# First V of the first batch in two groups of loads, and three zero blocks less ahead of the first scores

## The chip, the cores and the metric

The kernel runs on one NeuronCore of one Trainium2 chip. Its engines work side by side and meet through semaphores: TensorE (PE, with its weight loads listed as PEld) multiplies matrices, VectorE (DVE), ScalarE (ACT) and GpSimd (POOL) work on vectors, SyncE (SP) issues stores. Loads and stores are carried by 16 DMA engines; in this kernel POOL issues all loads and SP all stores. The metric is the time of one execution in microseconds (us) on the device, taken as the median of several runs.

## The reference

Two steps follow each other. Attention over 8 batches, 12 heads, 448 tokens and 64 numbers a head, and then a feed-forward layer over the 3584 tokens with 768 numbers each:

```
scores = scale * q @ k.T                  # per batch and head, scale = 1/sqrt(64)
attn   = softmax(scores)
x      = (attn @ v)  as [3584, 768]       # heads side by side
h      = x @ w_in                         # w_in 768 x 2048
g      = h * (1 / (1 + exp(-h)))
out    = g @ w_out                        # w_out 2048 x 768
```

The inputs and the output are 32-bit floats in memory. The loads turn the inputs into 16-bit floats on their way, the products take those and add up in 32 bits. Sizes of loads are given as they are written, in 16 bits.

## The kernel before

**Tiling.** A unit is one batch and one group of four heads (`HG = 4`, three groups a batch, `NG = 3`). For a unit the kernel loads K, Q and V, turns K and Q with VectorE's 32 x 32 transposes (lines 407, 412, 424), multiplies them to scores in 32-row strips of TensorE (`scores`, line 460), takes the exponential on ScalarE (`expo`, lines 505 and 516), and multiplies the exponentials with V and with ones (`attend_alone`, line 568, for the first units, line 582 later). VectorE turns and inverts the sums (lines 640, 648, 655) and scales the product into `xT` (lines 674 and 685), which is the left side of the feed-forward layer (`h<-xT,w_in_t`, line 697).

**Scores.** The scores of batch 0 come in bursts; each burst fills two score tiles of PSUM, and ScalarE takes one exponential for each. There are three such tiles at this stage, so a burst waits for the exponential that frees its tile.

**V.** All V of a batch lies in one tile `V` of 128 partitions by 12 heads by 4 chunks by 64. One load brings one quarter of the partitions, 32, for some heads, with 4 or 3 tokens in each partition, which is 64 or 48 KB for four heads (`load_v`, lines 351 to 366). `plan_v` queues four such loads, x = 0 to 3; for batch 0 they take all 12 heads at once (192 and 144 KB), for later batches one group of four heads. `lift_v` (lines 369 to 376) moves one chunk of the second group between partitions on VectorE, and clears what it came from; it needs the first two quarters of V.

**The order of the work.** A planner writes all instructions in a fixed order ahead of time. The class `Order` keeps a clock and an estimate for every engine, and emits an operation when its estimate says that it can start. `od.load` puts a load in POOL's list with its rows and bytes; when the planner reaches it, it calls the emit function that was given with it. Loads go out in the order in which they were planned (lines 1216 to 1243): K of unit 0, its Q in two halves, K and Q of unit 1, K of unit 2, then V of batch 0, Q of unit 2, K and Q of batch 1's first unit, six pieces of `w_in`, and so on. The planner holds at most eight loads in flight (`LOADS = 8`, line 23), and so does the program: a load waits on POOL for the landing of the load eight before it, because they share a semaphore.

**Zero blocks.** Where TensorE would wait at the start, the planner puts products of zeros (`run_zeros`, line 2329), which write to a spare bank and are read by nobody. The first group has `FIRST` blocks of 128 columns, four to a product; later groups are as long as the wait that the planner expects:

```
each = mm(128) if od.now > COLD else 0.107
n = max(1, int((wait - 0.06) / each), int(wait / each + 0.9) * (od.now < COLD))
wide = 4
if warm.pop("first", None):
    n, wide = FIRST, 4
```

Of the kernel before, what the change touches and what calls it, by code (L numbers as in the profile page):

```python
# [214 lines left out]
def kernel(  # L215
# [11 lines left out]
    B, NH, S, D = q.shape  # L227
# [3 lines left out]
    NG = NH // HG  # L231
# [15 lines left out]
    EAGER = 1  # L247
    HALVES = 0
    NEAR, LATE = 0.15, -0.3
    COLD, FIRST, QUIET = 8.5, 47, 0.16  # L250
    SHY = 0.5
    AWAIT = 1.0
    FAR = (NT * B // 4 - 1,)
# [86 lines left out]
    def form(b, hg):  # L340
        return "low" if b == 0 else ("low", "high")[(NG * b + hg) % 2]
# [9 lines left out]
    def load_v(b, hg0, hg1, x):  # L351
        if b not in VT:
            VT[b] = sb.tile([128, NH, NCH, D], FP16, name=f"V_{b}", tag="V", bufs=2)
        hs = slice(HG * hg0, HG * hg1)
        kind = form(b, hg0)
        if x == 0 and b > 0 and NG * b + hg0 < ALONE:
            lo = 64 if kind == "low" else 0
            nc.gpsimd.memset(VT[b][lo : lo + 64, hs, place(b, hg0, NCH - 1), :], 0.0)
        first, count = X_TOK[kind][x]
        at = int(kind == "high" and count < NCH)  # L360
        nc.gpsimd.dma_start(  # L361
            out=VT[b][32 * x : 32 * (x + 1), hs, at : at + count, :],
            in_=v[b, hs].rearrange("h (i g) d -> i h g d", g=TPP)[
                :, :, first : first + count, :
            ],
        )
# [88 lines left out]
    def place(b, hg, c):  # L455
        return (c + 1) % NCH if form(b, hg) == "high" else c
# [714 lines left out]
    od = Order(SHY)  # L1171
# [10 lines left out]
    def plan_q(n):  # L1182
# [7 lines left out]
            for g0, g1 in (PIECES if n == 0 else ((0, TPP),))  # L1190
        ]

    def plan_v(b, hg0, hg1):
        made = []
        for x in range(4):
            ring = v_ring if (x == 0 and hg0 == 0) else None
            heads, toks = HG * (hg1 - hg0), X_TOK[form(b, hg0)][x][1]
            made.append(
                od.load(32 * heads, 2 * D * toks, lambda x=x: load_v(b, hg0, hg1, x), ring)
            )  # L1200
        for hg in range(hg0, hg1):
            ld_v[(b, hg)] = made
# [16 lines left out]
    plan_q(1)  # L1219
    plan_k(0, 2)  # L1220
    plan_v(0, 0, NG)
    plan_q(2)
    plan_k(1, 0)
# [7 lines left out]
    plan_q(5)  # L1231
    plan_w_out(0, 4)
    plan_v(1, 0, 1)
    plan_w_out(4, 8)
    plan_w_out(8, 12)
    plan_v(1, 1, 2)
    plan_w_out(12, 16)
    plan_v(1, 2, 3)
    for n in range(NB0 + NG, NU):
        b, hg = units[n][:2]  # L1240
# [1186 lines left out]
```

## Time and profile before

| what | us |
|---|---|
| median of 3 runs | 377.55 (377.43 to 378.58) |
| profiled execution | 377.82 |
| its span | 376.0 |
| PE busy | 370.4 |
| DVE busy | 292.4 |
| ACT busy | 255.6 |
| POOL busy | 85.0 |

The span is the time from the first to the last instruction of the profiled execution; the execution's own time has some 1.8 us more around it. A line of the timeline or of the chain begins with the start and the duration in us, then the engine, the line of the kernel, the operation, what it writes and reads, and how often it was done in one stretch; the square bracket tells how long the engine sat idle before it, and what ended that. A row of a group has the busy time, the mean duration in ns, and the idle time before. `rk` and `room` are raw K, `rq` is raw and turned Q, `KT` is turned K, `s` the scores, `E` and `T` the exponentials, `a` the product with V or with ones, `z` the bank of the zero blocks and whatever takes it over, `rdn` the sums. A load has landed when all its 16 engines have reported; "to landing" counts from its issue on POOL.

### The profile page before, as it was taken

What the parts mean: (1) busy time and instruction counts of PE and PEld (TensorE: products, weight loads), DVE (VectorE), ACT (ScalarE), POOL (GpSimd) and SP (SyncE); (2) the same over time, 40 slices, a digit from 0 to 9 for tenths busy, and PEclk for the clock granted to TensorE, in tenths of its full rate; (3) what the DMA queues carried; (4) which work ended last, traced back from release to release, by engine and by line L of the source; (5) the groups of instructions that cost most, each with busy time, mean ns of one, the idle gap of its engine ahead of it and who ended that gap; (6) DMA issues with size and microseconds to landing.
All of it is one profiled execution on the core that took longest, in us unless ns stands there. A gap on an engine that the chain in (4) does not pass through costs nothing.

```text
span 376.0 us, 10031 instructions
## 1 busy us (share of the span) xinstructions
PE 370.4 (98%) x4052; PEld 189.3 (50%) x4052; DVE 292.4 (78%) x613; ACT 255.6 (68%) x402; POOL 85.0 (23%) x155
## 2 busy tenths in 40 slices
PE   8999999999999999999999999999999999999996
PEld 3365445444444444444444444545556765556774
DVE  3667958999995969995969998899579744648883
ACT  4988873887878788777878777658872238883121
POOL 7552437424016326006423200000000000000000
PEclk9999999999999999999999999999999999999999
DMA  7999999919049948147964421210001241000144
GB/s 112 198 208 210 206 204 183 199 18 135 14 99 137 171 51 120 30 94 106 171 97 57 60 53 45 53 34 0 0 3 46 63 107 39 0 3 26 50 115 150
DMA packets 35967, 34.49 MB, mean 92 GB/s; under 512 B 11856, under 2 KB 35152, under 8 KB 35920
## 3 DMA queue, kind: packets, MB, share of 16 engines
q0 software_dynamic: 25312, 22.82, 41.1%
q1 hardware_dynamic: 10064, 10.40, 10.2%
q8 instruction: 32, 0.52, 0.6%
q10 hardware_dynamic: 544, 0.62, 0.5%
q14 instruction: 15, 0.12, 0.1%
HBM read 45.61 MB, written 11.01 MB: 151 GB/s over the span
## 4 chain that ended last, share of the span: by engine, by line
PE 97%; DMA 1%; issue 0%; POOL 0%; DVE 0%; POOLq 0%
PE p L697 28%; PE h L697 21%; PE f L697 16%; PE s L460 12%; PE a L582 8%; PE o L697 3%; PE a L568 2%; PE n_Q L697 2%; PE a L615 2%; PE n_P L697 2%; DMA rq<-in_q_dram 1%; PE z L2329 1%; PE z L697 0%; PE z L568 0%; DVE ost L1033 0%
## 5 line engine op out<-in xcount | busy, mean ns | idle before, releaser
L516 ACT ACTIVATE E<-s 128x896 f16<-128x896 f32 x164 | 142.0, 919 | 24.8 <-PE s L460 24.7
L697 PE MATMUL h<-xT,w_in_t 128*32 128x448 f16 (+2 forms) x762 | 83.5, 348 | 0.0
L697 PEld LDWEIGHTS <-w_in_t 128*128 128x128 f16 (+1 forms) x909 | 54.6, 97 | 50.0 <-issue 8.1
L361 POOL DMA_DIRECT2D V<-in_v_dram x88 | 48.5, 565 | 49.7 <-PE a L582 29.2
L697 PEld LDWEIGHTS <-G 128*128 128x128 f16 (+1 forms) x652 | 40.1, 97 | 26.0 <-issue 5.0
L729 ACT ACTIVATE th<-h 128x448 f16<-128x448 f32 x67 | 36.6, 546 | 24.3 <-PE h L697 20.7
L697 PE MATMUL p<-w_out_t,G 128*128 128x384 f16 (+1 forms) x294 | 46.7, 327 | 0.0
L460 PE MATMUL s<-rq,KT 32*128 32x448 f16 (+3 forms) x728 | 44.9, 347 | 0.5 <-DVE rq L424 0.5
L697 PEld LDWEIGHTS <-S 128*128 128x128 f16 (+1 forms) x329 | 29.9, 98 | 21.3 <-issue 3.4
L773 DVE SCALAR_TENSOR_TENSOR G<-th,h 128x448 f16<-128x448 f16 (+1 forms) x64 | 35.7, 573 | 4.7 <-ACT th L729 4.3
L697 PE MATMUL p<-D,S 128*128 128x384 f16 (+1 forms) x217 | 39.3, 327 | 0.0
L1027 ACT COPY ost<-p 128x384 f32<-128x384 f32 x36 | 17.3, 480 | 26.8 <-PE p L697 24.2
L582 PE MATMUL a<-E,V 128*32 128x448 f16 (+1 forms) x640 | 32.7, 356 | 0.0
L685 DVE SCALAR_TENSOR_TENSOR xT<-a,rdn 128x448 f16<-128x448 f32 x46 | 26.9, 618 | 3.4 <-PE a L582 2.2
L338 POOL DMA_DIRECT2D rq<-in_q_dram x25 | 13.9, 558 | 67.0 <-PE s L460 58.2
L460 PEld LDWEIGHTS <-KT 32*128 32x128 f16 (+1 forms) x824 | 12.4, 96 | 31.0 <-issue 29.2
L529 DVE TENSOR_TENSOR T<-T,E 128x1792 f16<-128x1792 f16 x21 | 22.8, 1086 | 4.8 <-ACT E L516 4.8
L529 DVE TENSOR_TENSOR T<-E,E 128x1792 f16<-128x1792 f16 x21 | 22.7, 1082 | 4.1 <-ACT E L516 4.0
L901 DVE TENSOR_TENSOR p<-f,p 128x448 f32<-128x448 f32 x15 | 9.3, 623 | 20.3 <-PE f L697 13.9
L1049 DVE TENSOR_TENSOR ost<-p,ost 128x384 f32<-128x384 f32 x28 | 15.4, 552 | 12.2 <-ACT ost L1027 7.7
L697 PE MATMUL f<-sx,tw 128*128 128x448 f16 x102 | 23.7, 353 | 0.0
L582 PEld LDWEIGHTS <-V 128*32 128x32 f16 (+1 forms) x640 | 13.5, 95 | 18.0 <-issue 10.1
(140 smaller groups left out, 483.9 us busy)
## 6 DMA issues: line engine op xcount, KB each, us to landing
out_dram<-ost SPq DMA_DIRECT2D x146, 48.0 KB, 2.2
rk<-in_k_dram POOLq DMA_DIRECT2D x23, 224.0 KB, 5.3
rq<-in_q_dram POOLq DMA_DIRECT2D x23, 224.0 KB, 5.9
w_out_t<-in_moe_w_out_dram POOLq DMA_DIRECT2D x4, 768.0 KB, 12.6
V<-in_v_dram POOLq DMA_DIRECT2D x42, 64.0 KB, 4.4
out_dram<-wide SPq DMA_DIRECT2D x48, 48.0 KB, 1.6
V<-in_v_dram POOLq DMA_DIRECT2D x42, 48.0 KB, 4.6
w_in_t<-in_moe_w_in_dram POOLq DMA_DIRECT2D x6, 256.0 KB, 9.2
```

Source lines behind the costliest of these rows:

```text
L338: nc.gpsimd.dma_start(out=rawq[n][:, cols], in_=group_of(q, b, hg)[:, cols])
L361: nc.gpsimd.dma_start(out=VT[b][32 * x : 32 * (x + 1), hs, at : at + count, :], in_=v[b, hs].rearrange("h (i g) d -> i h g d", g=TPP)[:, : ...
L460: nc.tensor.matmul(out=pS[p0 : p0 + 32 * (x1 - x0), h % 2, at : at + q1 - q0], lhsT=KT[(b, hg)][32 * h : 32 * (h + 1), key_rows(b, hg, c, ...
L516: nc.scalar.activation(out=E[(n, w)][:, 2 * y : 2 * y + 2, :], in_=pS_t[(n, w, y)][:, :, 0:S], func=AF.Exp, scale=attn_scale,)
L529: nc.vector.tensor_tensor(out=T[n], in0=T[n] if step else E[(n, 0)], in1=E[(n, step + 1)], op=ALU.add,)
L582: nc.tensor.matmul(out=a[32 * h : 32 * (h + 1), 0:S], lhsT=VT[b][k0:k1, HG * hg + h, place(b, hg, c), part - 1 :: 2], rhs=e[k0:k1, h], sta ...
L685: nc.vector.scalar_tensor_tensor(out=x3(b, cc)[:, cc % 3, 32 * g0 : 32 * g1], in0=acc[(n, part)][:, 0:nq], scalar=0.5, in1=rdn_t[n].rearra ...
L697: nc.tensor.matmul(out=out[i : i + cut], lhsT=w[:, i : i + cut], rhs=x, start=start, stop=stop, skip_group_check=True,)
L729: nc.scalar.activation(out=th, in_=h_t[(b, f, t0)][:, 0:n], func=AF.Tanh)
L773: nc.vector.scalar_tensor_tensor(out=dst[:, f, at + lo : at + hi], in0=th_t[(b, f, t0)][:, lo - t0 : hi - t0], scalar=1.0, in1=h_t[(b, f, ...
L1027: nc.scalar.copy(out=ost(qd, *OUT[m]), in_=bank(qd, BANK[m]))
L1049: nc.vector.tensor_tensor(out=t, in0=bank(qd, BANK[m]), in1=t, op=ALU.add)
```

## The change

The planner still plans four loads of V for batch 0, with the old rows and bytes. What is emitted differs: the first four calls load only the first group of four heads, and the last of them then emits four more loads, for the other eight heads, one behind the other. So POOL issues eight loads where it issued four, with the same bytes and the same rows in all. Batches from 1 on are loaded as before.

The first group of zeros has 44 blocks instead of 47: eleven products of 512 columns instead of eleven and one of 384. Since the planner's clock moves, the next groups of zeros change by a block or so each, and one new product of 128 columns of zeros stands ahead of the first product with V, whose result now goes to the bank of those zeros. The order of everything else on TensorE, VectorE, ScalarE and SyncE is the same; on POOL the four loads come in behind the first four.

```diff
-    COLD, FIRST, QUIET = 8.5, 47, 0.16
+    COLD, FIRST, QUIET = 8.5, 44, 0.16
...
+    def in_turn(b, hg0, hg1, x):
+        if b:
+            return load_v(b, hg0, hg1, x)
+        load_v(0, 0, 1, x)
+        if x == 3:
+            for y in range(4):
+                load_v(0, 1, NG, y)
+
     def plan_v(b, hg0, hg1):
         made = []
         for x in range(4):
             ring = v_ring if (x == 0 and hg0 == 0) else None
             heads, toks = HG * (hg1 - hg0), X_TOK[form(b, hg0)][x][1]
             made.append(
-                od.load(32 * heads, 2 * D * toks, lambda x=x: load_v(b, hg0, hg1, x), ring)
+                od.load(32 * heads, 2 * D * toks, lambda x=x: in_turn(b, hg0, hg1, x), ring)
             )
```

## The prediction

> **What bounds the kernel now.** I read the page's engine shares first, then the chain of work that ended last, cut to its first 27 us because the edit lies there, then the timeline of that stretch.
>
> ```profile
> span 376.0 us, 10031 instructions
> PE 370.4 (98%) x4052; PEld 189.3 (50%) x4052; DVE 292.4 (78%) x613; ACT 255.6 (68%) x402; POOL 85.0 (23%) x155
> ...
> PE   8999999999999999999999999999999999999996
> ```
>
> TensorE (PE) is busy 98% of the span, and 75.80 of 75.80 us between 24.2 and 100 us. Before 24.2 us it is filled up with zero blocks and waits for others. So the edit is worth what it moves the start of the full stretch, at 24.2 us.
>
> The chain, from the first loads to the first expert product:
>
> ```profile
> 2.48 4.71 DMA rq<-in_q_dram
> ...
> 7.21 0.42 DVE rq L424
> ...
> 7.67 0.58 PE s L460 x16
> ...
> 13.93 0.75 PE s L460 x8
> 14.68 0.57 issue
> 15.25 0.94 PE a L568 x16
> 16.19 0.51 PE s L460 x7
> ```
>
> The chain does not pass the first zeros: it starts with the second half of the first Q, which lands at 7.18. Its one hole is the 0.57 us at 14.68, ahead of the first product with V. "issue" names no releaser, so I looked at who else woke then, in the timeline:
>
> ```profile
> 15.25 0.56 PE L568 MATMUL a<-T,V 128*32 128x448 f16 x8 [0.57 <-issue]
> 15.45 1.39 POOL L379 DMA_DIRECT2D w_in_t<-in_moe_w_in_dram  x2 [0.25 <-DMA V<-in_v_dram]
> ...
> 16.12 0.57 PE L460 MATMUL s<-rq,KT 32*128 32x448 f16 x8
> ...
> 16.73 3.35 ACT L516 ACTIVATE E<-s 128x896 f16<-128x896 f32 x4 [0.25 <-PE s L460]
> ...
> 18.19 0.64 DVE L407 STREAM_TRANSPOSE KT<-rk 128x192 f32<-128x192 f32 x2
> ...
> 18.89 0.65 DVE L424 STREAM_TRANSPOSE rq<-rq 128x448 f32<-128x448 f32 x1
> ...
> 20.58 3.35 ACT L516 ACTIVATE E<-s 128x896 f16<-128x896 f32 x4 [0.50 <-PE s L460]
> ```
>
> POOL waits for a load of V in the same moment. By issue plus time to landing the four loads of V land at 12.42, 13.48, 14.21 and 15.16: the last one ends the hole. ScalarE (ACT) is the true bound of this stage. Its exponentials start every 0.80 us without a hole from 6.66 to 15.47. Then they are late three times: 16.73 instead of 16.27 (0.46), 20.58 instead of 19.94 (0.64), 24.18 instead of 23.79 (0.39), 1.49 us in all.
>
> **The change part by part.** All times are of the profiled execution: span 376.05, 377.82 with what lies around it, 0.27 above the median of 377.55. I take the difference from the median.
>
> *Three zero blocks less.* Blocks of 128 columns take 0.107 us there (starts of 512 columns are 0.427 apart), so the zeros end at 5.69 instead of 6.01. The first scores wait for the first Q turned (5.42 + 0.41, and 0.05 for the semaphore): 5.88 instead of 6.04. That is 0.16 us for the first two exponentials. The third needs the second half of Q at 7.67 as before, and is already without slack (scores end at 8.25, ACT starts at 8.28). Worth 0; what hides it is that load. The later zero groups change by one block or less, ahead of scores that wait for ACT: 0.
>
> *V in eight loads.* The third K lands at 11.66. The nearest rows for pieces of four heads are the V pieces of batch 1 in the same full queue: a 768 KB weight load lands at 42.22 and 48, 48, 64 and 64 KB behind it at 42.49, 42.77, 43.11 and 43.47, 1.25 us for the four. So the first head group is there at 12.91, 2.25 us earlier. At worst each takes as long as the longest 192 KB load, 1.06, giving 15.90, a loss of 0.74 on the hole. I take 12.91: same bytes per row, same queue. The four pieces of eight heads are two thirds of the old 3.50 us (11.66 to 15.16), 2.33. Together 3.58: the queue behind V is 0.08 us later. V's last piece then lands at 15.24; the second head group is first multiplied at 18.97, and VectorE's (DVE) lift at 14.66 needs the first two big pieces, at about 14.1.
>
> *What the four extra issues push.* Every load waits for the landing of the one eight before it (0.29 us from landing to issue), and POOL needs 0.54 us for each. The big pieces issue at 7.47, 9.12, 10.22 and 11.95, behind the landings at 7.18, 8.83, 9.93 and 11.66. The third Q moves from 7.47 to 12.5, the next K from 9.40 to 13.05, the next Q from 10.22 to 13.6, the first w_in piece from 11.94 to 14.15, the sixth from 16.14 to 17.75. The K behind it still issues at about 18.7. Would they land late? The first load of all, with nothing ahead, took 3.54 us from issue to landing (1.26 to 4.80). So the third Q could be there at 16.0 (it landed at 15.72, and DVE takes it at 16.4), the K at 16.6 (landed 18.17) and the Q at 17.1 (landed 18.87). The queue ahead of them still decides, not the issue. Bounds: 0.08 late (queue time alone) to 0.3 late (third Q's 16.0 against 15.72, passed on to all behind); I take 0.08, since 1.5 us of slack stand on the two that matter.
>
> *The path.* The first scores of the second head group end at 14.68. A new 128-column zero block comes next (the 256-column block at 24.07 holds PE 0.12; I take 0.06, ends 0.05 and 0.12). V is there, so the product starts at 14.74 instead of 15.25. The scores behind it start at 15.61, and the exponential at 16.30 instead of 16.73: 0.43 won. What is late next? The scores at 19.83 need the K of batch 1 turned and its Q too. DVE starts these at 18.19 and 18.89, 0.02 behind their landings at 18.17 and 18.87. This Q is turned at 19.54, so the scores can't start before 19.59 (19.67 with the 0.08), instead of 19.83. From 0.43 there is 0.16 to 0.24 left. Behind it DVE is busy without a break until 22.28, when it frees the bank of the product at 22.47: that one wins 0.14 at most; the sums beside it keep 0.16 to 0.24 and feed the first expert product. From 24.2 us PE is full and hands the gain on whole.
>
> Sum: 0 + 0.43 - 0.19 to 0.27 for the landings - 0 to 0.10 for the bank = 0.06 to 0.24; I take 0.2, 377.35.
>
> **The rivals.**
>
> *The gain dies at the landings.* If each of the four extra loads costs the queue 0.08 to 0.15 us instead of 0.02, the K and Q of batch 1 land 0.3 to 0.6 us later than 18.17 and 18.87, and the scores at 19.83 start as before or up to 0.4 later: 377.5 to 377.95. For it: 0.02 us between landing and use, and issues 3 us later. Against it: a full queue, in which the small pieces of batch 1 cost no more than their bytes. The Trainium skill, "DMA: Bandwidth & Descriptors", section "Rules for kernel authors", speaks against the change: many small transfers should be merged, since below 64 KB one pays mostly overhead. By the 2.0 us a load that its section "Anatomy of one DMA" gives, four more loads would cost 8 us if nothing overlapped; the pieces of batch 1, 0.27 to 0.36 us apart, don't bear that out for queued loads.
>
> *All holes of ACT close.* If instead the K and Q come early (the K took 2.45 us behind the Q before it, and 1.1 us is usual for 224 KB here), the second and third hole may go too: 1.49 us, 376.06. Against it: the landings don't change their order, and DVE has no gap after 18.19.
>
> *Slower: the clock comes late.* The first zeros run at half speed:
>
> ```profile
> L2329 PE MATMUL z<-zeros 128*128 128x512 f16 x11 | 4.9, 632 | 1.0 <-DVE zeros L296 1.0
> ...
> L2329 PE MATMUL z<-zeros 128*128 128x512 f16 x3 | 1.0, 384 | 0.0
> ```
>
> The first row is up to 5.8 us, the second from 6.5 us: the clock doubled in between, some 5 us after the first zeros. With 44 blocks PE has a new gap from 5.69 to 5.88. If that holds the clock at half for t us longer, PE does half the work in t, and gets back at most the 0.51 us that it idles at 7.16: the loss is up to t / 2 - 0.5. From 1.4 us on it eats the 0.2; from 3.7 us on it passes 1.33 and the kernel is slower by over 0.3%. If the count of 5 us begins anew at 5.88, t is 5.0 and the loss 2.0: 377.55 - 0.2 + 2.0 = 379.35. Against it: the gap of 0.51 us at 7.16 and the one of 0.57 at 14.68 left the clock up, and 0.19 us is little beside 5. The Trainium skill, "TensorE: Matmul & The Clock Gate", section "What's actually happening", says that a free-running window of about 3.4 us must be busy before the clock is raised. By it a spoiled window would cost one more, a t of 3.4 and up to 1.2 us, 378.55 at most. The trace agrees that it rises after some 5 us of work, but no row tells how much of a gap is borne.
>
> **How the numbers follow.** Forecast (0.06 to 0.46 won, the upper end with the K and Q early): 0.50. Gain lost at the landings: 0.20. Clock late by less than 3.7 us: 0.11. All three are within 0.3% (1.13 us, about what a measurement of this kernel can tell from no change; the three runs shown spread 1.15): 0.81. All holes close: 0.08, faster. Clock held down longer: 0.11, slower. The range is 376.8 to 378.5: gains of 0.46 and losses of 0.4 around the median, and the runs' own spread (0.12 below it, 1.03 above, of which I take most); the two outer cases, 0.19, are left out.
>
> **What would show it.** Right: the first four V pieces land near 12.9; no hole at 14.68; ACT's second row starts near 16.3; DVE still takes the K at 18.2 and the scores start near 19.6; the first product with w_in starts 0.1 to 0.25 us before 24.19. Wrong: that K or Q landing past 18.5 and 19.2, the lift on DVE waiting for V past 14.7, the first product with V still waiting, or zeros of 512 columns at 630 ns after 6.5 us.

## The result, and the profile after

The changed kernel takes 379.03 us (median of 12 runs, 377.43 to 379.60); the kernel before took 377.47 beside it (12 runs, 377.23 to 378.58). The ratio is 1.0033, with a 95% interval of 1.0021 to 1.0045. The prediction was 377.35, in a range of 376.8 to 378.5, with a chance of 0.11 for slower. It is slower, and outside the range. The profiled execution of the changed kernel took 379.60, with a span of 377.8; that is the upper end of its runs, so the times below are of a loss of 1.8 us, the usual one being 1.6.

The page of the changed kernel shows the same work on TensorE in a longer span: 370.2 us busy, as before (370.4).

```profile
span 377.8 us, 10042 instructions
...
PE 370.2 (98%) x4054; PEld 189.8 (50%) x4054; DVE 292.5 (77%) x613; ACT 255.4 (68%) x402; POOL 87.0 (23%) x159
```

What was forecast for the hole came. In the timeline of the changed kernel the first product with V follows its zero block at once, at 14.64, and ScalarE (ACT) goes on without a hole to 17.98. Then come waits for loads that were not there before:

```profile
14.48 0.23 PE L2337 MATMUL z<-zeros 128*128 128x128 f16 x1
14.64 0.56 PE L568 MATMUL z<-T,V 128*32 128x448 f16 x8
...
17.31 0.65 DVE L424 STREAM_TRANSPOSE rq<-rq 128x448 f32<-128x448 f32 x1 [0.73 <-DMA rq<-in_q_dram]
...
18.01 0.57 PE L460 MATMUL s<-rq,KT 32*128 32x224 f16 x16 [0.97 <-ACT E L516]
...
18.62 1.73 ACT L516 ACTIVATE E<-s 128x896 f16<-128x896 f32 x2 [0.64 <-PE s L460]
...
18.73 0.64 DVE L407 STREAM_TRANSPOSE KT<-rk 128x192 f32<-128x192 f32 x2 [0.27 <-DMA rk<-in_k_dram]
...
19.80 0.65 DVE L424 STREAM_TRANSPOSE rq<-rq 128x448 f32<-128x448 f32 x1 [0.30 <-DMA rq<-in_q_dram]
...
24.89 1.31 PE L697 MATMUL z<-xT,w_in_t 128*128 128x224 f16 x12
...
39.07 0.55 PE L697 MATMUL h<-xT,w_in_t 128*128 128x448 f16 x2 [0.40 <-DMA w_in_t<-in_moe_w_in_dram]
```

VectorE (DVE) waits for the third Q until 17.31, and for the K and the Q of batch 1 until 18.73 and 19.80 (18.19 and 18.89 before). The first product with `w_in` starts at 24.89 instead of 24.19, and at 39.07 TensorE (PE) waits for the last piece of `w_in`, in a stretch in which it never waited before. (The wait at 18.01 is named after ACT, but the third Q, turned by 17.96, ended it: in a kernel with this Q early, `e1_loads` below, the same scores started at 17.19, while ACT's last two exponentials of that row were still running.)

The chain of work that ended last tells it in one view. Before, it was TensorE all the way from 7.67. In the changed kernel it goes from load to load. Up to 27 us:

```profile
4.03 6.97 DMA room<-in_k_dram
10.99 0.28 issue
11.28 0.46 POOL V L361
11.74 0.11 issue
11.85 5.44 DMA rq<-in_q_dram
17.28 0.28 issue
17.57 10.58 DMA w_in_t<-in_moe_w_in_dram
```

and behind that, up to 80 us:

```profile
28.43 15.88 DMA w_out_t<-in_moe_w_out_dram
...
44.59 1.61 POOL V L361 x3
46.20 11.83 DMA w_out_t<-in_moe_w_out_dram
...
64.37 7.13 DMA rq<-in_q_dram
...
71.53 0.65 DVE rq L424
...
77.72 2.43 PE h L697 x12
```

The third Q takes 5.44 us from its issue at 11.85. It was issued 2.7 us ahead of the landing of V's last piece (14.58). Before, it was issued 7.7 us ahead of it (7.47, 15.16). Fifteen of the 16 DMA engines were done with it by 15.72, the time at which all were done in the kernel before; the last one took until 17.28.

The last view is the load engines' rate. A line has a stretch, its length, then the busy time and the instructions of PE, PEld, DVE, ACT and POOL, the clock, the DMA share and GB/s. Before:

```profile
12.00:16.00 4.00, 3.43 (x50) 1.15 (x48) 2.24 (x8) 4.00 (x6) 3.31 (x5) 1.00 1.32 203
16.00:20.00 4.00, 4.00 (x85) 1.75 (x80) 3.55 (x8) 3.75 (x5) 1.93 (x4) 1.00 1.21 205
20.00:24.00 4.00, 4.00 (x128) 2.28 (x120) 3.17 (x9) 3.42 (x5) 2.11 (x3) 1.00 1.24 206
```

and in the changed kernel:

```profile
8.00:12.00 4.00, 3.90 (x37) 1.39 (x35) 2.17 (x7) 4.00 (x6) 1.87 (x4) 1.00 1.32 189
12.00:16.00 4.00, 4.00 (x59) 1.39 (x57) 1.97 (x6) 4.00 (x6) 4.00 (x7) 1.00 1.15 156
16.00:20.00 4.00, 3.03 (x68) 1.42 (x64) 2.70 (x7) 3.36 (x5) 2.20 (x4) 1.00 1.08 150
20.00:24.00 4.00, 3.63 (x112) 2.26 (x104) 3.64 (x8) 3.42 (x5) 2.01 (x4) 1.00 1.24 205
```

From 12 to 20 us the loads move (156 + 150) x 4 us = 1.22 MB instead of (203 + 205) x 4 = 1.63 MB. The 0.41 MB that are missing are 2.0 us at 205 GB/s, and every later landing up to the first `w_out` piece is late: third Q 17.28 (15.72), K 18.71 (18.17), Q 19.77 (18.87), first `w_in` piece 21.07 (20.15), ninth 39.03 (36.25), first `w_out` piece 44.31 (42.22). TensorE takes this up in steps. Its instructions start 0.61 us earlier than before at 15.25, but later by 0.51 at 17.5, 0.63 at 24.65, 1.20 at 37.9, 1.48 at 56.6, 1.68 at 73 and 1.86 at 75.9, and 1.82 at the end.

So two questions were open: which part of the change slows the loads, and why TensorE, which never waited between 24 and 100 us, pays for nearly all of it.

### The profile page after: what moved, and what is told of

Read it like the earlier page. It is cut to its first block, busy times and chain, and to the rows that moved or that the text cites. A ratio compares the mean times of both kernels' runs of the same rounds, so it can differ in the third digit from the quotient of the medians.

```text
span 377.8 us, 10042 instructions
## 1 busy us (share of the span) xinstructions
PE 370.2 (98%) x4054; PEld 189.8 (50%) x4054; DVE 292.5 (77%) x613; ACT 255.4 (68%) x402; POOL 87.0 (23%) x159
## 4 chain that ended last, share of the span: by engine, by line
PE 78%; DMA 15%; POOL 3%; DVE 2%; issue 1%; POOLq 0%
PE p L697 28%; PE f L697 16%; PE h L697 14%; PE s L460 8%; PE a L582 7%; DMA w_out_t<-in_moe_w_out_dram 7%; DMA rq<-in_q_dram 3%; DMA w_in_t<-in_moe_w_in_dram 3%; PE n_Q L697 2%; DMA room<-in_k_dram 2%; PE a L615 2%; PE n_P L697 2%; POOL V L361 2%; POOL rk L330 1%; POOL rq L338 1%
## 5 line engine op out<-in xcount | busy, mean ns | idle before, releaser
L361 POOL DMA_DIRECT2D V<-in_v_dram x92 | 50.6, 562 | 52.4 <-PE a L582 29.2
L1027 ACT COPY ost<-p 128x384 f32<-128x384 f32 x36 | 17.3, 480 | 26.8 <-PE p L697 19.2
L460 PEld LDWEIGHTS <-KT 32*128 32x128 f16 (+1 forms) x824 | 12.5, 96 | 31.8 <-issue 29.3
L685 DVE SCALAR_TENSOR_TENSOR xT<-a,rdn 128x448 f16<-128x448 f32 x45 | 26.1, 616 | 2.8 <-PE a L582 2.3
L582 PEld LDWEIGHTS <-V 128*32 128x32 f16 (+1 forms) x640 | 13.6, 95 | 18.0 <-issue 10.5
```

The source lines that it names most:

```text
L361: nc.gpsimd.dma_start(out=VT[b][32 * x : 32 * (x + 1), hs, at : at + count, :], in_=v[b, hs].rearrange("h (i g) d -> i h g d", g=TPP)[:, : ...
L460: nc.tensor.matmul(out=pS[p0 : p0 + 32 * (x1 - x0), h % 2, at : at + q1 - q0], lhsT=KT[(b, hg)][32 * h : 32 * (h + 1), key_rows(b, hg, c, ...
L582: nc.tensor.matmul(out=a[32 * h : 32 * (h + 1), 0:S], lhsT=VT[b][k0:k1, HG * hg + h, place(b, hg, c), part - 1 :: 2], rhs=e[k0:k1, h], sta ...
L685: nc.vector.scalar_tensor_tensor(out=x3(b, cc)[:, cc % 3, 32 * g0 : 32 * g1], in0=acc[(n, part)][:, 0:nq], scalar=0.5, in1=rdn_t[n].rearra ...
L1027: nc.scalar.copy(out=ost(qd, *OUT[m]), in_=bank(qd, BANK[m]))
```

## The experiments

My theory, formed from these traces, was this: a load waits for the landing of the one eight before it; four extra loads take four of these eight places; so the loads behind V are issued late, too little is in flight, and the rate falls. The rivals: the small V pieces cost the load engines more than their bytes; the third Q alone is the trouble, whose landing is first late; POOL's time for four more issues (2.2 us) does it; and the zeros.

The median of before, measured beside each group of experiments, was 377.64 (first four), 377.63 (next four) and 377.69 (last three); all those 71 runs lie between 377.19 and 379.00.

**The two parts alone.** `e1_loads` has the eight loads and 47 zero blocks, `e2_zeros` the four loads and 44.

```diff
# e1_loads, against the changed kernel      # e2_zeros, against before
-    COLD, FIRST, QUIET = 8.5, 44, 0.16     -    COLD, FIRST, QUIET = 8.5, 47, 0.16
+    COLD, FIRST, QUIET = 8.5, 47, 0.16     +    COLD, FIRST, QUIET = 8.5, 44, 0.16
```

> The change's eight loads of V, but 47 zero blocks as before. Slots theory (the four extra loads take four of the eight places in flight, so the third Q and all behind it are issued some 4 us later, the DMA queue runs shallow from 12 us on and its rate falls from about 205 to about 150 GB/s): nearly the whole loss is here, 1.0 to 1.8 us slower than before, third Q landing past 16.8 us. Zeros theory (the shorter first zeros bring the loss through the clock): within 0.3 us of before.

> 44 zero blocks, V in four loads as before. Slots theory: within 0.3 us of before. Zeros theory: 1.0 to 1.8 us slower.

Measured: `e1_loads` 379.18 us (378.36 to 380.26), ratio 1.0041 (1.0028 to 1.0054); `e2_zeros` 377.71 (377.32 to 378.20), ratio 1.0001 (0.9992 to 1.0009). The loads are the whole loss, and the zeros cost nothing. In `e1_loads` the rate is 166 and 159 GB/s in the two stretches from 12 to 20 us, in `e2_zeros` 205 and 204. One thing that I had expected did not come: issued at 11.68, the third Q of `e1_loads` landed at 15.60, not past 16.8, and ahead of the 15.72 of before. The K and the Q behind it were late all the same, at 18.38 and 19.47. So the loss does not need a late third Q.

**Loads without bytes.** V goes in four loads as before, and behind them stand four loads of 1 KB.

```diff
+    def in_turn(b, hg0, hg1, x):
+        load_v(b, hg0, hg1, x)
+        if b == 0 and x == 3:
+            for y in range(4):
+                nc.gpsimd.dma_start(
+                    out=w_out_t[0:32, NFF - 1, 16 * y : 16 * (y + 1)],
+                    in_=v[0, 0, 32 * y : 32 * (y + 1), 0:16],
+                )
```

> V in four loads as before, and behind them four tiny loads of 1 KB each, which go into a corner of w_out_t that the real load overwrites later. They take four places in flight and carry nothing. Slots theory: third Q lands past 16.8 us as in the changed kernel, and the kernel is 0.8 to 2.2 us slower, since the loss comes without the early V. Pieces theory (small pieces of V cost the DMA engines more than their bytes): V and third Q land as before (15.2 and 15.7), within 0.3 us of before.

Measured: 380.34 us (379.31 to 380.58), ratio 1.0064 (1.0052 to 1.0076). V lands as before (12.43 to 14.98), and the third Q is issued at 12.71. The windows of this kernel:

```profile
12.00:16.00 4.00, 3.88 (x53) 1.30 (x52) 1.68 (x5) 4.00 (x6) 2.36 (x5) 1.00 1.09 132
16.00:20.00 4.00, 3.95 (x83) 1.75 (x80) 2.36 (x6) 4.00 (x5) 3.47 (x5) 1.00 1.02 143
20.00:24.00 4.00, 2.57 (x72) 1.58 (x65) 3.46 (x8) 2.15 (x4) 2.00 (x4) 1.00 1.17 183
```

So the way in which V's bytes are cut is not what costs: four loads that bring next to nothing cost 2.7 us by the medians (2.4 by the ratio), more than V's eight loads, and more than the 2.2 at most that I had written; the third Q landed at 16.77. They take the same places and put still fewer bytes into them.

**The third Q first.** The third Q is issued right behind the first head group's four pieces, the other four pieces of V behind it; VectorE's lift moves behind the turn of this Q.

```diff
+    def next_q(n, g0, g1):
+        load_q(n, g0, g1)
+        if n == 2:
+            for y in range(4):
+                load_v(0, 1, NG, y)
...
+    def turn_next(n, g0, g1):
+        turn_q(n, g0, g1)
+        if n == 2:
+            lift_v(0)
+            lift_v(1)
```

> V's first head group in four loads, then the third Q, then the four loads of the other eight heads; VectorE's lift behind the turn of that Q; 47 zero blocks. Slots theory: the third Q is issued near 7.5 and lands near 14.5, so the hole at 16 to 18 us is gone; the K and Q of batch 1 are still issued past 12 us and land 0.3 to 1 us late; 0.2 us faster to 0.8 us slower than before. If the loss were due to the third Q alone, it would be 0.2 to 0.5 us faster than before.

Measured: 379.43 us (378.45 to 380.89), ratio 1.0038 (1.0025 to 1.0051). The third Q lands at 13.74, but the K is issued at 12.47 and lands at 19.17, the Q at 20.22, with 153 and 156 GB/s. One load put right does not help: what is issued behind V is late. The loss, 1.4 us by the ratio and 1.8 by the medians, is also larger than the 0.8 at most that I had written from the places.

**POOL's time without loads.** Four memsets of 128 x 512 in the place of the four extra loads, and then nine.

```diff
+    def in_turn(b, hg0, hg1, x):
+        load_v(b, hg0, hg1, x)
+        if b == 0 and x == 3:
+            for y in range(4):          # 9 in e9_delay
+                nc.gpsimd.memset(w_out_t[:, NFF - 1, 0:512], 0.0)
```

> V in four loads as before, 47 zero blocks; in the place of the four extra loads GpSimd does four memsets of 128 x 512 (into a corner of w_out_t that is loaded later), some 0.5 us each, so as much of its time as four issues. The theory of the places (a load waits for the landing of the one eight before it, and four extra loads take four of the eight) expects little: the third Q issues at 9.6 instead of 7.47, but the next K and Q at 10.1 and 10.7 and the first w_in at 11.94 as before, DMA above 195 GB/s from 12 to 20 us, and 377.4 to 377.9. If GpSimd's time is what costs (the 1 KB loads gave 380.34), the kernel comes out at 379 or more.

> V in four loads as before, 47 zero blocks, no extra load; nine memsets of GpSimd (0.55 us each) behind the fourth load of V hold back what comes next until it issues at the times of the changed kernel: the third Q at about 12.0 (11.85 there), the next K at 12.6, the next Q at 13.1, w_in from 13.7. If the late issue alone does it (the four places cost by delaying the issues, and by nothing else), the DMA rate falls below 180 GB/s between 12 and 20 us, the K of batch 1 lands behind 18.5 and the time is 378.5 to 379.7. If the extra loads themselves slow the queue, all stays near before: 377.4 to 378.0.

Measured: `e5_pool` 377.69 us (377.39 to 378.04), ratio 1.0003 (0.9995 to 1.0012); `e9_delay` 379.64 (378.92 to 380.41), ratio 1.0050 (1.0035 to 1.0065). With four memsets the third Q is issued at 9.31, the K at 9.86, and the rate stays up. The windows of `e5_pool`:

```profile
12.00:16.00 4.00, 3.78 (x58) 1.26 (x56) 1.97 (x5) 4.00 (x6) 3.02 (x5) 1.00 1.29 203
16.00:20.00 4.00, 3.84 (x96) 1.71 (x88) 3.43 (x9) 3.71 (x5) 1.77 (x3) 1.00 1.22 204
```

So 2.2 us of POOL's time cost nothing here. With nine memsets the third Q is issued at 12.21, the K at 12.77 and the Q at 13.30, 0.37 us behind the times of the changed kernel, and there is no extra load at all. The windows of `e9_delay`:

```profile
12.00:16.00 4.00, 4.00 (x54) 1.31 (x53) 1.53 (x5) 4.00 (x7) 4.00 (x8) 1.00 1.16 157
16.00:20.00 4.00, 3.98 (x76) 1.73 (x79) 3.72 (x9) 4.00 (x6) 3.02 (x5) 1.00 1.04 148
20.00:24.00 4.00, 4.00 (x128) 2.29 (x127) 3.27 (x8) 3.49 (x5) 1.50 (x3) 1.00 1.23 199
```

156 and 150 in the changed kernel, 157 and 148 here: late issue alone is enough for a loss of this size, without any extra load. That the extra loads have no price beside it is not shown. One thing came out otherwise than I had written: the K landed at 17.93, not behind 18.5, and PE is within some 0.2 us of before from 16 to 37 us. It then loses 0.28 us at 37.9, another 0.73 at 40.5 and 0.21 at 56.6. The first and the last step are waits for weights, pieces of `w_in` and `w_out` that landed at 38.10 and 57.77 (36.25 and 55.99 before). The middle one is named after VectorE (`G` and `X` hold the g of the reference):

```profile
41.50 1.29 PE L697 MATMUL h<-xT,w_in_t 128*128 128x448 f16 x6 [0.56 <-DVE G L773]
```

VectorE had first to turn a Q that landed at 40.27 (38.45 before). So in this execution the whole loss comes behind 37 us, through the late weights and through the late Q of a later unit.

**Fewer extra loads.** V in six loads (the first two quarters whole, the last two cut), in five (only the last quarter cut), and two loads of 1 KB instead of four.

```diff
+    def in_turn(b, hg0, hg1, x):
+        if b or x < 2:                  # x < 3 in e8_five
+            return load_v(b, hg0, hg1, x)
+        load_v(0, 0, 1, x)
+        if x == 3:
+            for y in range(2, 4):       # range(3, 4) in e8_five
+                load_v(0, 1, NG, y)
```

> V in six loads: the first two quarters for all twelve heads, the last two for the first head group, then these two for the other eight heads; 47 zero blocks. Two extra loads instead of four. The first head group should be there at about 14.2 (11.66 and 480 of 672 KB at the old rate of 3.50 us), so the hole of 0.57 us at 14.68 closes as in the changed kernel. By the places the loss is about half of that of the eight loads (379.18): 378.0 to 378.7, and the DMA rate from 12 to 20 us lies between 160 and 205 GB/s. If the loss came from having V's first group early (other pieces displaced, not places), it would be as in the eight loads, 379 or more; if two places are free to give, 377.0 to 377.4.

> V in five loads: three quarters for all twelve heads, the last one for the first head group and then for the other eight; 47 zero blocks. One extra load. The first head group is there at about 14.7, so the hole at 14.68 just closes. By the places a quarter of the loss of the eight loads or less, against at most 0.2 us won by the hole: 377.3 to 377.9. If the first place is already as dear as the mean of the four 1 KB loads (0.7 us) the time is 377.9 to 378.3; if the gain of the hole comes through whole, 377.0 to 377.3, which would beat both kernels.

> V in four loads as before, 47 zero blocks; two extra loads of 1 KB behind V instead of four. If each place costs the same, half of the loss of four (1.0064): 1.003, some 379.0. If there is an edge (as long as enough bytes are in flight nothing is lost, below it all of it), the loss is either under 0.1% or, in some runs and not in others, up to that of four, with a spread of 2 us or more as with V in six loads (377.33 to 381.17).

Measured:

| kernel | extra loads | median, us | range, us | ratio (95%) |
|---|---|---|---|---|
| `e8_five` | 1 | 377.44 | 377.30 to 379.55 | 1.0001 (0.9990 to 1.0013) |
| `e7_six` | 2 | 378.23 | 377.33 to 381.17 | 1.0027 (1.0007 to 1.0046) |
| `e10_two` (1 KB) | 2 | 377.65 | 377.32 to 380.60 | 1.0016 (0.9998 to 1.0034) |
| `e1_loads` | 4 | 379.18 | 378.36 to 380.26 | 1.0041 (1.0028 to 1.0054) |
| `e3_slots` (1 KB) | 4 | 380.34 | 379.31 to 380.58 | 1.0064 (1.0052 to 1.0076) |

One extra place cost nothing that these runs show. With two, the runs fall apart: of 12 runs of `e10_two`, seven lie between 377.32 and 377.78 and five between 378.59 and 380.60; of `e7_six`, four are below 377.6 and five above 378.9, up to 3.5 us above before. So the price is not so much for each load. There is an edge, and two extra loads stand on it. Both profiled executions were among the undisturbed runs, and show what went with it: the third K landed early, at 10.37 and 10.17 (11.66 in before's, 10.66 to 11.12 in the kernels that lost), the third Q was issued at 9.35 and 9.25, and the rate from 12 to 20 us was 189 GB/s or more. No disturbed run of these two was profiled, so what decides between the two outcomes stays open. The windows of `e7_six`:

```profile
12.00:16.00 4.00, 4.00 (x61) 1.28 (x64) 2.10 (x6) 4.00 (x6) 3.53 (x6) 1.00 1.27 207
16.00:20.00 4.00, 3.78 (x94) 1.75 (x96) 3.93 (x10) 3.48 (x5) 2.70 (x5) 1.00 1.21 196
```

Its first product with V starts at 14.36, 0.89 us before that of before, but of that only 0.28 us are left at TensorE's end, and `e5_pool`, whose V is not early, has 0.20 there. In `e8_five` the product starts at 14.92 without a hole, and the ratio shows nothing won.

**The same extra loads where the queue is deep.** The four loads of 1 KB stand behind the ninth piece of `w_in`.

```diff
+    def w_in_then(c, f0, f1):
+        load_w_in(c, f0, f1)
+        if f1 == DFF and c == NG - 1:
+            for y in range(4):
+                nc.gpsimd.dma_start(...)     # as in e3_slots
```

> V in four loads as before, 47 zero blocks; the four extra loads of 1 KB, which cost 2.7 us behind V, are issued behind the ninth piece of w_in instead, where the loads in flight are of 224 to 768 KB instead of 48 to 224 KB. If what costs is that the four loads left in flight hold too few bytes to keep the DMA engines busy, they do at this place, four of them being more than 1.5 MB: w_out's first piece lands less than 0.5 us after 42.22, and 377.4 to 378.2. If an extra load has a price of its own wherever it stands (0.7 us each), w_out lands 2 us or more later and the time is 379 to 380.3.

Measured: 378.08 us (377.52 to 378.74), ratio 1.0012 (1.0003 to 1.0021). In place of 2.7 us they cost 0.45. They land some 0.18 us apart at 35.8 to 36.4, and the rate from 24 to 40 us is 208 GB/s. The Trainium skill, "DMA: Bandwidth & Descriptors", section "Rules for kernel authors", says that below 64 KB one pays mostly overhead. The trace agrees that 0.18 us for 1 KB is all overhead, but four of these are 0.7 us, and `e3_slots` lost 2.7: the overhead of a small load is the smaller part of what it did.

**What a late stream of weights costs.** Two loads of 192 KB more behind the ninth piece of `w_in`, where the queue is deep: 384 KB, or 1.9 us at 205 GB/s, of nothing but bytes.

```diff
+    def w_in_then(c, f0, f1):
+        load_w_in(c, f0, f1)
+        if f1 == DFF and c == NG - 1:
+            load_w_out(12, 13)
+            load_w_out(13, 14)
```

> V in four loads as before, 47 zero blocks; behind the ninth piece of w_in two loads of 192 KB more, which bring two eighths of the last quarter of w_out early, to be loaded once more at their own place. The queue is deep there, so they cost the DMA engines their bytes, 384 KB or 1.9 us at 205 GB/s, and no dry queue. If the stream of weights leaves TensorE no slack up to 75 us, so that what the queue lost before 20 us is paid whole at the later waits, the kernel is slower by 1 to 1.9 us: 378.6 to 379.5. If TensorE has slack behind 24 us and only the start of the full stretch counts, it stays within 377.4 to 378.0.

Measured: 379.28 us (378.08 to 380.93), ratio 1.0043 (1.0026 to 1.0060), which is 1.6 us (377.69 x 0.0043) for 1.9 us of bytes. The timeline of this kernel on TensorE:

```profile
40.75 1.29 PE L697 MATMUL h<-xT,w_in_t 128*128 128x448 f16 x6 [0.65 <-DVE G L773]
57.22 1.48 PE L697 MATMUL o<-w_out_t,G 128*32 128x384 f16 x32 [0.20 <-DMA w_out_t<-in_moe_w_out_dram]
74.60 2.43 PE L697 MATMUL h<-xT,w_in_t 128*128 128x448 f16 x12 [0.92 <-DVE X L773]
```

The wait at 57.22 is for a piece of `w_out`. The other two are named after VectorE, which had first to turn a Q that landed at 39.52 and at 71.44 (38.45 and 68.85 before). The changed kernel's later steps come in the same two ways: at 39.07 it waits for the ninth piece of `w_in`, at 58.08 it starts 0.05 us behind the landing of a piece of `w_out`, and the step at 73 us comes from a Q that landed at 71.50 and reached TensorE by way of VectorE, as the chain above shows. So the loads have little slack behind 24 us, though no wait of TensorE showed it before.

## Why the prediction was wrong

- **Three zero blocks: worth 0.** Right, by `e2_zeros` (1.0001). The rival of the late clock did not come. In the profiled execution of the changed kernel, zeros of 512 columns took 385 ns between 6.4 and 12 us:

```profile
L2337 PE MATMUL z<-zeros 128*128 128x512 f16 x6 | 2.0, 385 | 0.0
```

There the clock had risen before the new gap (381 ns for the zeros that start at 4.67), so this execution does not test what the gap does. `e2_zeros` does: its zeros took 634 ns up to the gap and 384 between 6.4 and 12 us.

- **V's first group early, and the hole of 0.57 us closed.** Right. The four pieces landed by 12.17 (forecast 12.91, the rest being a third K that landed 0.67 us earlier), 1.18 us behind that K for 1.25 forecast; all eight took 3.59 us for 3.58. The product started at 14.64 (14.74), the lift on VectorE at 14.54 without a wait, and ACT's hole at 16.7 went.
- **"The queue ahead of them still decides, not the issue."** This is the step that failed. The issues came about where I had put them (third Q 11.85 for 12.5, K 12.40 for 13.05, Q 12.93 for 13.6), but not the landings: 17.28 for 15.8, 18.71 for 18.25, 19.77 for 18.95. I took the price of a late issue from the first load of all, 3.54 us to landing, and asked for each load by itself whether that was in time. For one load that price was not far off: the third Q took 3.91 us in `e1_loads` and 3.71 in `e9_delay`, and of the 5.44 here all beyond 3.87 is one DMA engine of the 16. But the K behind it took 5.2 to 6.3 us in these three, the Q 5.7 to 6.8, and the slow rate went on until 20 us, although by 13.45 the Q, the K, the next Q and a piece of `w_in` were all issued. What the sum needed was a rate, 150 to 160 GB/s instead of 205 for eight microseconds, or 2.0 us; I had 0.08 for it, and 0.3 as its bound. Of the traces it could have been suspected in before's first microseconds: its rate was 103 to 142 GB/s from 4.8 to 7.2 us, with seven to ten loads issued, and it reached 200 only at 12.8 us.
- **K and Q of batch 1 eat part of the gain.** The mechanism was right, the size was not. I gave them 0.02 us behind the landing, and they took all of it: K 0.54 and Q 0.91 later than before (0.21 and 0.60 in `e1_loads`). This is the rival "the gain dies at the landings", with its mark (K past 18.5, Q past 19.2), but it allowed 0.4 us of loss at most.
- **"From 24.2 us PE is full and hands the gain on whole."** It held for a gain (`e7_six` is 0.27 us early at 26 us and 0.28 at the end), but not for a loss, and it is why the rival came out too small too. At 24.65 the loss was 0.63 us; from there on it grew to 1.82, at 38, 56 and 73 us, behind the last `w_in` piece, a piece of `w_out` and a late Q. That TensorE was never idle had said only that nothing was late, and not by how much. The slack could have been read as landing against first use: in before the `w_out` piece landed at 55.99, and TensorE came to it at 56.60, 0.61 us later. In the changed kernel it landed at 58.03, 2.04 later; less 0.61 that is 1.43, and TensorE was 1.48 late. `e9_delay` (57.77) and `e11_bytes` (57.18) give 1.17 and 0.58 in the same way, and TensorE was 1.22 and 0.62 late there.
- **The range.** For the landings it took in 0.4 us of loss, from the rival that priced each extra load at up to 0.15 us of queue time; the bound of 0.3 in the sum came from the 3.54 us. Both are prices of single loads and know no rate, so the range fell with the step. The measured 379.03 lies between the 378.55 and the 379.35 of the late clock, which the range left out; that is chance, since the clock was not late. By the Trainium skill, "DMA: Bandwidth & Descriptors", section "Specifications", the first byte of a load issued by GpSimd moves after about 1 us; as an estimate from that, a third Q whose issue on POOL ended at 12.42 would start at some 13.4, in time for the end of V at 14.58. `e1_loads` agrees: there the third Q landed 1.19 us behind V's last piece, about the 1.1 us that 224 KB take at 205 GB/s. In the changed kernel its first engine was done at 15.05 and its last at 17.28. Neither says anything of the rate of what comes behind.

How late may an issue be? These are the profiled executions in order of the time from the third Q's issue to the landing of the last load ahead of it:

| kernel | issue of the third Q | last load ahead lands | between | GB/s, 12 to 16 and 16 to 20 us |
|---|---|---|---|---|
| before | 7.47 | 15.16 | 7.7 | 203, 205 |
| `e8_five` | 9.36 | 15.20 | 5.8 | 203, 184 |
| `e5_pool` | 9.31 | 14.79 | 5.5 | 203, 204 |
| `e10_two` | 9.25 | 14.13 | 4.9 | 203, 189 |
| `e7_six` | 9.35 | 14.04 | 4.7 | 207, 196 |
| `e3_slots` | 12.71 | 15.68 | 3.0 | 132, 143 |
| changed | 11.85 | 14.58 | 2.7 | 156, 150 |
| `e1_loads` | 11.68 | 14.41 | 2.7 | 166, 159 |
| `e9_delay` | 12.21 | 14.49 | 2.3 | 157, 148 |

In these nine executions, one of each kernel, the rate breaks somewhere between 3.0 and 4.7 us, though not sharply: `e8_five`, profiled in one of its longer runs (378.27), fell to 164 GB/s later, from 20 to 24 us. (`e4_qfirst` has the third Q early and is left out; its K is issued 4.3 us ahead of V's last landing, at 153 and 156 GB/s.) Why the slow rate lasts some eight microseconds, with four to eight loads issued, stays open; the runs show that it does, and that late issue is enough to bring it on.

No kernel here beats the one before. The hole that the change closes can be closed with one extra load (`e8_five`) and with two, but the time at the end does not fall.

## What to carry to other kernels

Count the loads in flight as a budget: when each load waits for the landing of the one eight before it, a load that is split in two takes a place from a later load, and the later load is issued late by as much as the small one is waited for. Ask of each moved issue not only whether that load lands in time, but how long before the landing of the last load ahead of it the issue comes (4.7 us kept the rate here, 3.0 did not); if too late, price all that follows at the lower rate (150 instead of 205 GB/s, for eight microseconds here). And an engine that is never idle does not prove slack in what feeds it: set the landing of each large load against its first use, and carry a delay of the stream on to the last of them, and through the engine that prepares what it brings (here VectorE, which turns Q).

## What the runs showed of the hardware

When the loads behind V were issued late, the rate did not come back at once: in five kernels (the changed one, `e1_loads`, `e3_slots`, `e4_qfirst`, `e9_delay`) they moved 132 to 166 GB/s for eight microseconds instead of 205. The last of these has no extra load. A load has landed when its slowest DMA engine is done: of the third Q, 15 engines were done at 15.72 and the last at 17.28. A load of 1 KB costs 0.18 us in a deep queue, and four of them 2.7 us of the kernel where they hold places. Near the edge the same kernel takes 377.3 or 380.6 us from run to run (`e10_two`): where its profiled execution was undisturbed, the third K had landed 1.5 us earlier than in before's, and 0.5 to 1.0 earlier than in the kernels that lost.
